# A fused block-causal attention and SoLU layer: two landing places for raw W_in, the gain taken into W_out's split, and 1/z by a diagonal matrix

## The chip, the cores and the metric

One core of one Trainium2 chip runs the whole program. The metric is device time in microseconds, the median of several executions. The engines are TensorE (PE, its weight loads PEld), VectorE (DVE), ScalarE (ACT), GpSimd (POOL), and SyncE (SP), which here only issues DMAs.

## The reference

Two stages, all inputs float32 (the launch hands W_in, W_out and g_ln over as float64 words, so their raw loads are twice as large):

```
scores = q @ k^T / 8                       # 8 batches x 8 heads, 576 x 576, head size 64
scores = where(query_block >= key_block, scores, -1e9)     # blocks of 64
attn   = exp(scores - max); attn = attn / (sum(attn) + 1e-9)
x      = attn @ v                          # heads side by side: 4608 tokens x 512
h      = x @ W_in                          # 512 x 1024
solu   = h * softmax(h)
ln     = (solu - mean) / sqrt(var + 1e-6) * g_ln
out    = ln @ W_out                        # 1024 x 512
```

## The kernel before

**Work.** Attention runs over 32 pairs of heads (four pairs a batch). Batch 0 is cut in two: part 0 (queries and keys 0 to 255, line 506 on) for its four pairs, then part 1 (the rest), so that the first 256 tokens are ready early. The program's pairs 0 to 3 are part 0, 4 to 7 part 1, 8 to 35 the other seven batches. The token stage runs over 36 tiles of 128 tokens: `moe` multiplies by W_in (24 matmuls, L798), forms the SoLU and the layer norm on DVE, ACT and POOL (the first vector step is the maximum at L804), and multiplies by W_out (24 matmuls, L863), after the rows have been transposed and split (`ch`, and the remainder `cl`, L855 for the first tiles). Every float32 operand of a large matmul is split into a high and a low part (`xh`, `xl`, `wih`, `wil`, `woh`, `wol`, `qh`, `ql`, `kh`, `kl`), and three matmuls stand for one.

**A pair.** Scores (L617, L623) land in PSUM, DVE takes the negative row maximum (`nm`, L652), ACT takes the exponential with its row sum `z` (L664), DVE forms `rz` = 1/z (L674, L675), and each block of `pb` is multiplied by it (L682 POOL, L683 DVE, L684 ACT: whichever the planner picks). Pairs 0 to 7 (`PEP`) then transpose `pb` on TensorE (L604) into PSUM, and it is copied out to `pt` (L464, L465); later pairs transpose on DVE and by DMA. The product with v is L710.

**Weights.** `prep` (L406 on) takes W_in and W_out apart, 512 columns at a time. One raw load of two pieces lands in `ub` (L402 for W_in, L398 for W_out), and each piece goes through about nine steps: low word to float (L414), clamp (L416 DVE, L417 POOL), scale (L418 to L420), shift and merge of the words (L421, L422), an add (L423, L424), for W_out the product with g_ln (L426), the high part (L429, L430), the remainder (L431, L432). All sixteen pieces share `ub`, so a load waits until both pieces of the one before it have been read. `qz` and `kz`, the landing places of q and k for later pairs, hold parts of batch 0's v and of its k and q at first, so their first loads (L511) wait for part 0's last product with v and for the first transposes.

**Order.** `Schedule` is a planner inside the program: each operation has modelled durations, alternatives on other engines and a due time made of the table `PARAMS`, and a list scheduler writes out one fixed order for each engine before anything runs. Every engine then executes its own list strictly in that order, waiting on semaphores; SP's list of DMAs too. Where the planner sees TensorE without work before 125 us of its own clock it puts in filler transposes of the identity (L352).

## Time and profile before

| | us |
|---|---|
| median of 3 runs (lowest, highest) | 707.98 (704.84, 710.37) |
| the profiled execution | 709.96 |
| its span, first to last instruction | 707.8 |
| TensorE busy in the span | 681.5 |
| VectorE, ScalarE, GpSimd busy | 553.1, 478.9, 368.7 |

The profiled execution is one run, 2.0 us above the median. Its span is 2.2 us shorter than its time. "Busy" on TensorE counts the fillers too, and matmuls overlap in their pipeline.

### The profile page before, as it was taken

What the parts mean: (1) busy time and instruction counts of PE and PEld (TensorE: products, weight loads), DVE (VectorE), ACT (ScalarE), POOL (GpSimd) and SP (SyncE); (2) the same over time, 40 slices, a digit from 0 to 9 for tenths busy, and PEclk for the clock granted to TensorE, in tenths of its full rate; (3) what the DMA queues carried; (4) which work ended last, traced back from release to release, by engine and by line L of the source; (5) the groups of instructions that cost most, each with busy time, mean ns of one, the idle gap of its engine ahead of it and who ended that gap; (6) DMA issues with size and microseconds to landing.
All of it is one profiled execution on the core that took longest, in us unless ns stands there. A gap on an engine that the chain in (4) does not pass through costs nothing.

```text
span 707.8 us, 14535 instructions
## 1 busy us (share of the span) xinstructions
PE 681.5 (96%) x4888; PEld 541.7 (77%) x4888; DVE 553.1 (78%) x1211; ACT 478.9 (68%) x1180; POOL 368.7 (52%) x591
## 2 busy tenths in 40 slices
PE   6888899999999899999999999999999999999997
PEld 5776777777777678777777777787878778888885
DVE  1889999996887888989798979898989883444442
ACT  2787998786676868686777767777777773444432
POOL 1247757647474465556555555655555543444432
PEclk9899999999999999999999999999999999999999
DMA  8944568969698889889898979798979766223121
GB/s 166 210 121 94 116 120 146 169 144 175 152 177 200 170 189 180 195 176 185 189 193 180 194 173 198 182 185 189 190 184 173 189 153 140 70 64 90 61 75 45
DMA packets 223435, 109.76 MB, mean 155 GB/s; under 512 B 186496, under 2 KB 202368, under 8 KB 223360
## 3 DMA queue, kind: packets, MB, share of 16 engines
q1 hardware_dynamic: 222320, 108.56, 74.8%
q8 instruction: 39, 0.64, 0.4%
q10 hardware_dynamic: 1040, 0.26, 0.2%
q14 instruction: 36, 0.29, 0.1%
HBM read 37.23 MB, written 9.44 MB: 66 GB/s over the span
## 4 chain that ended last, share of the span: by engine, by line
PE 66%; DVE 9%; DMA 9%; ACT 7%; issue 3%; SPq 3%; POOL 3%; DVEq 0%; POOLq 0%; ACTq 0%
PE ps L798 24%; PE ps L863 23%; PE ps L710 9%; PE ps L623 7%; DMA ub<-in_moe_w_in_dram 4%; ACT pb L664 3%; PE ps L617 2%; DVE nm L652 2%; DVE pb L690 2%; DMA kz<-in_k_dram 1%; DMA ct<-zb 1%; ACT pb L684 1%; SPq L511 1%; DMA vr<-in_v_dram 1%; DVE qz L582 1%
## 5 line engine op out<-in xcount | busy, mean ns | idle before, releaser
L664 ACT ACTIVATE pb<-ps,nm 128x512 f32<-128x512 f32 (+4 forms) x288 | 156.7, 563 | 44.2 <-DVE nm L652 43.7
L652 DVE TENSOR_REDUCE nm<-ps 128x1 f32<-128x512 f32 (+4 forms) x288 | 130.6, 504 | 0.1
L682 POOL TENSOR_SCALAR pb<-pb,rz 128x256 f32<-128x256 f32 (+4 forms) x106 | 60.2, 582 | 109.5 <-DVE rz L675 57.2
L690 DVE STREAM_TRANSPOSE pb<-pb 128x1536 f32<-128x1536 f32 (+1 forms) x56 | 102.9, 1838 | 9.5 <-ACT pb L684 6.7
L684 ACT ACTIVATE pb<-pb,rz 128x384 f32<-128x384 f32 (+4 forms) x171 | 91.4, 608 | 9.4 <-DVE rz L675 8.0
L710 PEld LDWEIGHTS ps<-pt,vr 128*64 128x64 f32 x1648 | 80.2, 137 | 19.3 <-issue 9.5
L710 PE MATMUL ps<-pt,vr 128*64 128x128 f32 (+1 forms) x1648 | 92.6, 269 | 0.0
L798 PE MATMUL ps<-wih,xh 128*128 128x512 f32 x288 | 82.9, 410 | 0.4 <-DVE ub L806 0.4
L863 PE MATMUL ps<-woh,ch 128*128 128x512 f32 x288 | 81.7, 405 | 0.0
L798 PE MATMUL ps<-wil,xh 128*128 128x512 f32 x288 | 79.3, 397 | 0.0
L863 PE MATMUL ps<-wol,ch 128*128 128x512 f32 x288 | 78.7, 395 | 0.0
L798 PE MATMUL ps<-wih,xl 128*128 128x512 f32 x288 | 78.7, 395 | 0.0
L863 PE MATMUL ps<-woh,cl 128*128 128x512 f32 x288 | 78.7, 395 | 0.0
L623 PE MATMUL ps<-kh,qh 64*128 64x128 f32 (+3 forms) x256 | 54.5, 385 | 12.0 <-ACT pb L664 9.1
L863 PEld LDWEIGHTS ps<-woh,ch 128*128 128x128 f32 x288 | 51.9, 188 | 18.5 <-issue 6.6
L798 PEld LDWEIGHTS ps<-wil,xh 128*128 128x128 f32 x288 | 54.8, 190 | 13.0
L863 PEld LDWEIGHTS ps<-wol,ch 128*128 128x128 f32 x288 | 54.2, 188 | 12.9
L798 PEld LDWEIGHTS ps<-wih,xl 128*128 128x128 f32 x288 | 54.2, 188 | 12.8
L863 PEld LDWEIGHTS ps<-woh,cl 128*128 128x128 f32 x288 | 54.2, 188 | 12.8
L798 PEld LDWEIGHTS ps<-wih,xh 128*128 128x128 f32 x288 | 52.2, 190 | 15.0 <-DVE ub L806 0.9
L841 ACT ACTIVATE ch<-ct 128x512 fp32r<-128x512 f32 x62 | 37.7, 624 | 36.6 <-DMA ct<-zb 31.6
L664 ACT ACTIVATION_READ_ACCUMULATOR pb<-ps,nm 128x1 f32 x288 | 60.8, 211 | 0.0
(123 smaller groups left out, 1284.2 us busy)
## 6 DMA issues: line engine op xcount, KB each, us to landing
pt<-pb SPq DMA_DIRECT2D x112, 400.0 KB, 6.2
ct<-zb SPq DMA_DIRECT2D x124, 128.0 KB, 2.6
out_dram<-ob SPq DMA_DIRECT2D x36, 256.0 KB, 2.6
vr<-in_v_dram SPq DMA_DIRECT2D x64, 128.0 KB, 4.0
kz<-in_k_dram SPq DMA_DIRECT2D x56, 144.0 KB, 3.9
qz<-in_q_dram SPq DMA_DIRECT2D x56, 144.0 KB, 4.5
ub<-in_moe_w_in_dram SPq DMA_DIRECT2D x8, 512.0 KB, 6.5
ub<-in_moe_w_out_dram SPq DMA_DIRECT2D x16, 256.0 KB, 3.2
```

The costliest lines, as they stand in the source:

```text
L511: SP.dma_start(dst[32 * g : 32 * g + 32].rearrange("p m (g d) -> p (m g) d", d=32), src[b0, ha + g - g % 2 : ha + g - g % 2 + 2, :, 32 * ( ...
L617: PE.matmul(t[:, 192 + k0 : 192 + k1], w_, x_[:, k0:k1], start=n_ == 0, stop=n_ == 2)
L623: PE.matmul(PS(sps[h])[:, off : off + 128 * (i_ + 1)], w_[half[h], 128 * i_ : 128 * i_ + 128], x_[half[h], 0 : 128 * (i_ + 1)], start=n_ = ...
L652: op("DVE", t_dve(wid[u]), lambda sp=sp, off=off, u=u: DVE.tensor_reduce(out=nm_[u], in_=PS(sp)[:, off : off + wid[u]], axis=AX.X, op=ALU. ...
L664: ACT.activation(dst, src, AF.Exp, bias=nm_[u], accum_out=z_[zg][:, zc : zc + 1])
L682: op("POOL", 0.836 * nn + 243, lambda b=b, zg=zg, zc=zc: POOL.tensor_scalar(out=puv(pb, b, pep), in0=puv(pb, b, pep), scalar1=rz_[zg][:, z ...
L684: ("ACT", t_act(nn, 133), lambda b=b, zg=zg, zc=zc: ACT.activation(puv(pb, b, pep), puv(pb, b, pep), AF.Copy, scale=rz_[zg][:, zc : zc + 1 ...
L690: op("DVE", 1.058 * 128 * (s1 - s0) + 86, lambda s0=s0, s1=s1: DVE.transpose(pb[:, :, s0:s1, :], pb[:, :, s0:s1, :]), r=[("P", i, b) for b ...
L710: PE.matmul(dst(PS(av)[half[h]]), w_, pt_[:, a0:a1, sl, :], start=start, stop=stop)
L798: PE.matmul(o_, a_[:, c, :], w_[:, c, s_], start=(si == 0 and c == 0), stop=(si == 2 and c == NKI - 1))
L841: op("ACT", t_act(512, 150), lambda c_=c_, h_=h_: ACT.activation(h_, c_, AF.Copy), r=["ct"], w=[("ch", hf)], key=key + K["ce"], alts=[("PO ...
L863: PE.matmul(o_, a_[:, c, :], w_[:, c, :], start=(hf == 0 and si == 0 and c == 0), stop=(hf == 1 and si == 2 and c == 7))
```

## The change

Three edits, and a new table of planner numbers.

1. Raw W_in loads go in turn to `ub` and to a second place, the slots 12 to 19 of the two `pb` buffers (which part 1 fills later). W_in's pieces take turns among four sets of temporaries (two of them in `pb` and `pt`) in place of two. The new table gives the last half of W_in the first due time.
2. The product with g_ln is no step of its own: the high part of W_out is written with the scale g_ln, and the remainder is T1 * g_ln - high in one instruction.
3. For pairs 0 to 7 the blocks of `pb` are no longer multiplied by 1/z. A matrix `dg` with 1/z on its diagonal is made per block row (identity times broadcast 1/z, L702 of the new file, on DVE or POOL), and TensorE's transposes become float32 matmuls with `dg` as the moving operand (L620 of the new file).

Beside these, part 1 no longer transposes q of the first 256 rows (four matmuls fewer a pair, and copies of 256 columns for 512).

```diff
+DGP = tuple(range(8))
...
 PARAMS = {
...
+    "x": 854.098, "h0": -147.594, "hs": 1139.434, "h": -51.86, "he": -142.998, "c": 105.783, "sq": -2.995,
+    "ct": -113.19, "ce": 111.289, "o": 2480.877, "oe": 4.124, "w0": 952.251, "w1": -125.07, "q32": 126.658,
...
-    wtmp = [(zb[:, 0:512], zb[:, 512:1024], ob[0]), (ctf[:, 0:512], ctf[:, 512:1024], ob[1])]
...
+    wtmp += [[(pbf[i][:, 20:24], [("P", i, LAST)])] + [(ptb[i][:, :, c : c + 4].rearrange("p b s n -> p b (s n)"), [("pt", i, s_) for s_ in range(c, c + 4)]) for c in (12, 16)] for i in range(2)]
...
-    raws = ub2.bitcast(U32)
+    raws = [x.bitcast(U32) for x in (ub2, pball[:, :, 12 * P : 20 * P])]
+    rawk = [[[("ub", i)] for i in range(2)], [[("P", i, (h, 3)) for h in range(2)] for i in range(2)]]
...
+        j_ = i // 2 % 2 if gcol is None else 0
+        dst, ks = raws[j_], rawk[j_]
...
-            op("SP", nd_ * 640, lambda: fetch(raws, src), w=[("ub", 0), ("ub", 1)], key=key, tail=1550, dma=3000)
+            op("SP", nd_ * 640, lambda: fetch(dst, src), w=ks[0] + ks[1], key=key, tail=1550, dma=3000)
...
+        scale = 1.0 if gcol is None else gcol
+        op("ACT", 520 if gcol is None else 613, lambda: ACT.activation(hi, T1f, AF.Copy, scale=scale), r=k1 + ([] if gcol is None else ["gt"]), w=[(name, "h")], key=key,
...
+            op("DVE", 602, lambda: DVE.scalar_tensor_tensor(out=lo, in0=T1f, scalar=gcol, in1=hi.bitcast(F32), op0=ALU.mult, op1=ALU.subtract), r=k1 + ["gt", (name, "h")], w=[(name, "l")], key=key, port=True)
...
-                    PE.transpose(PS(pt)[:, (s_ - c0) * P : (s_ - c0 + 1) * P], pb[:, s_, :], ident)
+                    o_ = PS(pt)[:, (s_ - c0) * P : (s_ - c0 + 1) * P]
+                    if diag:
+                        u = next(u for u in bs if soff[u] <= s_ <= soff[u] + u[1])
+                        PE.matmul(o_, pb[:, s_, :], dg[:, dcol(u), :], start=True, stop=True)
...
+                        eng.tensor_tensor(out=dg[:, d0 : d0 + n_, :], in0=ident[:, None, :].to_broadcast([P, n_, P]), in1=rz_[zg][:, z0 : z0 + n_, None].to_broadcast([P, n_, P]), op=ALU.mult)
...
-                for b in bs:
+                for b in () if diag else bs:
```

The built programs show how the orders move. On SP, from the sixth row of the program on, before:

```order
L402 DMA ub_125<-in_moe_w_in_dram 64x2x1024 x2
L398 DMA gt_76<-in_moe_g_ln_dram 32x8x1 x4
L522 DMA vr0_80<-in_v_dram 128x4x64 x2
L526 DMA vr0_80<-in_v_dram 64x2x64
L522 DMA vr1_81<-in_v_dram 128x4x64 x2
L526 DMA vr1_81<-in_v_dram 64x2x64
L402 DMA ub_125<-in_moe_w_in_dram 64x2x1024 x2
L484 DMA xt1_119<-in_k_dram 128x8x64
L484 DMA xt2_120<-in_q_dram 128x8x64
L484 DMA xt1_119<-in_k_dram 128x8x64
```

and of the change, from its twelfth row (the first rows are the same loads of q, k and v; `vr` and the first two of these k and q loads stand ahead of what is shown):

```order
L493 DMA xt1_118<-in_k_dram 128x8x64
L493 DMA xt2_119<-in_q_dram 128x8x64
L493 DMA kz_79<-in_k_dram 64x8x64
L493 DMA kz_79<-in_q_dram 64x8x64
L407 DMA pb_88<-in_moe_w_in_dram 64x2x1024 x2
L403 DMA gt_76<-in_moe_g_ln_dram 32x8x1 x4
L407 DMA ub_124<-in_moe_w_in_dram 64x2x1024 x2
L407 DMA pb_88<-in_moe_w_in_dram 64x2x1024 x2
L521 DMA qz_78<-in_q_dram 32x36x32 x4
L407 DMA ub_124<-in_moe_w_in_dram 64x2x1024 x2
L521 DMA kz_79<-in_k_dram 32x36x32 x4
L403 DMA ub_124<-in_moe_w_out_dram 32x2x1024 x4
```

The first load of W_in has moved behind the loads of v and behind all of batch 0's q and k; the second and third follow it at once; the fourth stands behind the first load into `qz`. On DVE, where it first meets W_in (before: its steps at L420 and L421 stand between part 0's first maxima):

```order
L652 TENSOR_REDUCE nm0_01_93<-ps5_66 128x1
L560 TENSOR_TENSOR kl0_85<-ps4_65,kh0_84 128x256
L465 TENSOR_SCALAR qh0_82<-ps4_65 128x256
L652 TENSOR_REDUCE nm0_00_92<-ps5_66 128x1
L561 SCALAR_TENSOR_TENSOR ql0_83<-ps4_65,qh0_82 128x256
L420 TENSOR_SCALAR ct_127<-ct_127 128x512
L421 TENSOR_SCALAR zb_126<-zb_126 128x512
```

and of the change:

```order
L702 TENSOR_TENSOR dg_135<-ident_67,rz1_0_115 128x512
L666 MEMSET ps5_66 64x2x64
L666 MEMSET ps2_63 64x2x64
L670 TENSOR_REDUCE nm0_01_92<-ps5_66 128x1
L670 TENSOR_REDUCE nm0_00_91<-ps5_66 128x1
L670 TENSOR_REDUCE nm0_11_96<-ps2_63 128x1
L670 TENSOR_REDUCE nm0_10_95<-ps2_63 128x1
L425 TENSOR_SCALAR pt1_90<-pb_88 128x4x128
L692 TENSOR_SCALAR z0_0_109,zsum_134<-z0_0_109 128x4
L693 RECIPROCAL rz0_0_113<-z0_0_109 128x4
```

DVE now takes the maxima of three of part 0's pairs before its first step on W_in (L425), not of half a pair; the third pair's 1/z stands right behind that step. On TensorE, at the first matmuls with W_in, before:

```order
L623 MATMUL ps2_63<-kl0_85,qh0_82 128x512
L623 MATMUL ps5_66<-kl0_85,qh0_82 128x512
L710 MATMUL ps4_65<-pt0_90,vr0_80 64x128 x6
L710 MATMUL ps3_64<-pt0_90,vr0_80 64x2x2x32 x8
L710 MATMUL ps3_64<-pt0_90,vr0_80 64x64 x10
L798 MATMUL ps0_61<-wih_72,xh0_121 128x512 x4
```

and of the change:

```order
L641 MATMUL ps4_65<-kl0_85,qh0_82 128x384
L641 MATMUL ps2_63<-kl0_85,qh0_82 128x384
L620 MATMUL ps3_64<-dg_135,pb_88 128x128 x3
L620 MATMUL ps5_66<-dg_135,pb_88 128x128 x3
L825 MATMUL ps1_62<-wih_72,xh0_120 128x512 x4
```

The first tile's matmuls stand behind the products with v of pair 4 alone, where they stood behind those of pairs 4, 5 and 6. Over the whole program TensorE's list has 73 fillers for 141, 88 transposes of q and k (L547) for 104, and 100 matmuls with `dg` for 100 transposes. Ahead of the first matmul with W_out (L863, now L890) it has one group of L617 (six matmuls), six of 512 columns and six of 256 columns of L623, and 26 of L710 fewer than before.

## Rows read from the trace of the kernel before

**Rows 1.** The page: the span, busy time (share) and instructions of the engines, and TensorE in 40 slices of the span, tenths busy.
```profile
span 707.8 us, 14535 instructions
PE 681.5 (96%) x4888; PEld 541.7 (77%) x4888; DVE 553.1 (78%) x1211; ACT 478.9 (68%) x1180; POOL 368.7 (52%) x591
...
PE   6888899999999899999999999999999999999997
...
```

**Rows 2.** Busy time by stretch: from and to, length, then for each engine busy us and instructions, then the granted clock of TensorE, the DMA engines' share and GB/s.
```profile
0.00:24.00 24.00, 15.80 (x130) 13.91 (x131) 9.42 (x30) 8.69 (x24) 5.04 (x16) 0.87 0.88 172
24.00:99.00 75.00, 66.32 (x673) 54.43 (x671) 67.25 (x193) 65.78 (x173) 43.50 (x64) 0.95 0.54 129
99.00:146.00 47.00, 45.09 (x357) 35.17 (x356) 45.47 (x101) 37.64 (x99) 29.61 (x43) 1.00 0.91 149
146.00:250.00 104.00, 100.65 (x751) 79.12 (x750) 84.58 (x188) 72.11 (x182) 58.76 (x96) 0.98 0.84 170
250.00:600.00 350.00, 349.81 (x2539) 275.93 (x2538) 301.20 (x652) 252.55 (x635) 192.02 (x316) 1.00 0.91 183
```

**Rows 3.** TensorE's fillers in the view by line: instructions, busy us and mean ns, idle time before them and what ended it; and from the timeline of TensorE (start, us) the first matmuls with W_out.
```profile
L352 PE MATMUL ps<-ident 128*128 128x128 f32 x141 | 21.2, 304 | 1.4 <-ACT pb L664 1.4
...
145.33 1.19 PE L863 MATMUL ps<-woh,ch 128*128 128x512 f32 x4
```

**Rows 4.** The chain of waits from 0 to 50 us: start, us, what. The first and the last of the four transfers of W_in.
```profile
6.79 9.69 DMA ub<-in_moe_w_in_dram
...
38.08 6.30 DMA ub<-in_moe_w_in_dram
```

**Rows 5.** Busy time by stretch as in rows 2, for the first 40 us and for DVE's stretch.
```profile
0.00:20.00 20.00, 11.80 (x111) 10.03 (x113) 5.43 (x17) 5.72 (x14) 2.86 (x14) 0.94 0.86 162
20.00:40.00 20.00, 18.84 (x174) 16.42 (x174) 17.12 (x55) 16.46 (x50) 6.33 (x6) 0.89 0.85 191
24.00:134.00 110.00, 99.41 (x922) 80.25 (x921) 101.95 (x267) 96.28 (x250) 69.33 (x101) 0.97 0.65 136
```

**Rows 6.** Timeline of DVE: start, us, instruction. The end of part 0's eighth maximum with the 1/z behind it, and the first remainder `cl` of a token tile.
```profile
24.16 0.18 DVE L675 RECIPROCAL rz<-z 128x4 f32<-128x4 f32 x1
...
133.53 0.68 DVE L855 TENSOR_TENSOR cl<-ps,ch 128x512 fp32r<-128x512 f32 x1
```

**Rows 7.** DVE's rows by line and form from 0 to 140 us: busy us and mean ns of one.
```profile
L652 DVE TENSOR_REDUCE nm<-ps 128x1 f32<-128x384 f32 x14 | 7.3, 545 | 0.0
...
L423 DVE CUSTOM_DVE_ANT_0 zb<-zb,ob 128x1024 uint16<-128x1024 uint16 x6 | 4.6, 765 | 0.0
...
L579 DVE SCALAR_TENSOR_TENSOR ql<-ps,qh 128x512 fp32r<-128x512 f32 x4 | 2.7, 680 | 0.0
...
L683 DVE TENSOR_SCALAR pb<-pb,rz 128x256 f32<-128x256 f32 x3 | 1.9, 642 | 0.0
L683 DVE TENSOR_SCALAR pb<-pb,rz 128x384 f32<-128x384 f32 x2 | 1.7, 851 | 0.0
...
L561 DVE SCALAR_TENSOR_TENSOR ql<-ps,qh 128x256 fp32r<-128x256 f32 x4 | 1.7, 415 | 0.0
...
L431 DVE TENSOR_TENSOR wol<-ct,woh 128x512 fp32r<-128x512 f32 x2 | 1.4, 696 | 0.0
...
L683 DVE TENSOR_SCALAR pb<-pb,rz 128x640 f32<-128x640 f32 x2 | 1.2, 610 | 0.0
```

**Rows 8.** Timeline of TensorE: twelve and thirteen transposes of `pb`, and sixteen records (eight matmuls, two records each) of batch 0's q and k transposes by plain float32 matmul with what follows them.
```profile
74.77 1.47 PE L604 MATMUL ps<-ident,pb 128*128 128x128 f32 x12
76.17 0.49 PE L623 MATMUL ps<-kh,qh 64*128 64x384 f32 x2
...
59.49 1.09 PE L537 MATMUL ps<-ident,xt 128*64 128x128 f32 x16 [1.36 <-ACT pb L664]
60.41 0.39 PE L537 MATMUL ps<-ident,kz 128*64 128x128 f32 x4
```

**Rows 9.** The chain of waits from 300 to 321 us: start, us, what.
```profile
315.80 2.90 PE ps L710 x52
318.70 1.01 PE ps L623 x12
319.72 0.99 PE ps L617 x6
```

**Rows 10.** Timeline of SP (start, us of issuing) and of TensorE: part 0's last product with v, and the first load into `qz` behind it.
```profile
76.94 0.92 PE L710 MATMUL ps<-pt,qz 128*64 128x128 f32 x12
...
77.89 2.99 SPq L511 DMA_DIRECT2D qz<-in_q_dram  x4
```

**Rows 11.** TensorE from 22 to 28 us: busy time by stretch (columns as in rows 2), and from its timeline the fillers.
```profile
22.00:24.00 2.00, 2.00 (x11) 2.00 (x10) 1.99 (x10) 1.54 (x7) 2.00 (x2) 0.50 1.01 215
24.00:26.00 2.00, 2.00 (x19) 2.00 (x18) 0.59 (x5) 0.93 (x6) 0.34 (x1) 0.91 1.14 214
26.00:28.00 2.00, 2.00 (x21) 2.00 (x19) 1.98 (x6) 1.97 (x6) 0.00 (x0) 1.00 1.23 278
...
20.61 7.59 PE L352 MATMUL ps<-ident 128*128 128x128 f32 x51
```

More of the change, by code (lines that the diff above doesn't have):

```diff
@@ L315 @@
     PAD = 8
-    pbt = [sb(f"pb{i}", [4, NSL * 32 + PAD]) for i in range(2)]
+    pball = sb("pb", [2, 4 * (NSL * 32 + PAD)])
+    pbt = [pball[:, i].rearrange("p (r n) -> p r n", r=4) for i in range(2)]
     pbs = [x[:, :, 0 : NSL * 32].rearrange("p r (s i) -> p r s i", i=32) for x in pbt]
@@ L416, in prep @@
-        op("DVE", 335, lambda: DVE.tensor_scalar(out=T2, in0=high, scalar1=TOP, scalar2=-TOP, op0=ALU.min, op1=ALU.max), r=[kr_], w=[k2], key=key, port=True,
+            op("SP", nd_ * 640, lambda: fetch(dst, src), w=ks[0] + ks[1], key=key, tail=1550, dma=3000)
+        high = raw[:, :, :, 1].bitcast(F32)
+        op("ACT", 570, lambda: ACT.activation(T3.bitcast(I32), raw[:, :, :, 0], AF.Copy, scale=2.0**-29), r=kr, w=k3, key=key,
+           alts=[("POOL", 640, lambda: POOL.tensor_scalar(out=T3.bitcast(I32), in0=raw[:, :, :, 0], scalar1=2.0**-29, scalar2=1.0, op0=ALU.mult, op1=ALU.mult), K["a_t3"])])
@@ L423, in prep @@
[L423 removed]
+        op("DVE", 335, lambda: DVE.tensor_scalar(out=T1.bitcast(U32), in0=T2.bitcast(U32), scalar1=3, scalar2=0x7FFFFFF8, op0=ALU.logical_shift_left, op1=ALU.bitwise_and), r=k2, w=k1, key=key, port=True)
+        op("DVE", 602, lambda: DVE.scalar_tensor_tensor(out=T1.bitcast(U32), in0=T2.bitcast(U32), scalar=0x80000000, in1=T1.bitcast(U32), op0=ALU.bitwise_and, op1=ALU.bitwise_or), r=k1 + k2, w=k1, key=key, port=True)
@@ L424, in prep @@
+        op("DVE", 602, lambda: DVE.tensor_tensor(out=T1.bitcast(I32), in0=T1.bitcast(I32), in1=T3.bitcast(I32), op=ALU.add), r=k1 + k3, w=k1, key=key, port=True,
            alts=[("POOL", 1225, lambda: POOL.tensor_tensor(out=T1.bitcast(I32), in0=T1.bitcast(I32), in1=T3.bitcast(I32), op=ALU.add), K["a_ai"])])
-        if gcol is not None:
-            op("ACT", 613, lambda: ACT.activation(T1, T1, AF.Copy, scale=gcol), r=[k1, "gt"], w=[k1], key=key,
-               alts=[("POOL", 588, lambda: POOL.tensor_scalar(out=T1, in0=T1, scalar1=gcol, scalar2=1.0, op0=ALU.mult, op1=ALU.mult), K["a_cg"]),
-                 ("DVE", 400, lambda: DVE.tensor_scalar(out=T1, in0=T1, scalar1=gcol, scalar2=None, op0=ALU.mult), K["a_lf"])], port=True)
@@ L565, in trans @@
             def trans(x, ps, tail):
-                for c in range(4):
-                    block(ps, c * P, raw0[x][:, 512 * c :])
+                for c in range(4 if tail else 2):
+                    block(ps, c * P, raw0[x][:, 512 * (c if tail else c + 2) :])
                 if tail:
```

64 lines of the change are left out of this document (37 added, 27 removed), and 11 rows, old and new, of the table PARAMS.

## The prediction

> **What bounds the kernel now.** I read the page first: TensorE is busy for 681.5 of 707.8 us, and its slices are full from about a fifth of the span on [rows 1]. The view by stretch says where it is not: from 250 to 600 us it is busy 349.81 of 350, but up to 146 us it lacks 8.2 + 8.7 + 1.9 = 18.8 us, and 3.4 more from 146 to 250 [rows 2]. Of the busy time before 146 us another 21.2 us are fillers, which compute nothing [rows 3]. So from the first matmul with W_out at 145.33 us [rows 3] the kernel is a list of TensorE work executed almost without a hole, and before it some 40 us of TensorE's time go by without program work. Everything that this change can win lies there; later, more load on DVE, ACT or POOL costs nothing while TensorE stays the last to be ready.
>
> What holds the start is the next view. In the chain of waits the first 44 us are four transfers of W_in into the one landing place, the first ending at 6.79 + 9.69 = 16.5 us, the last at 38.08 + 6.30 = 44.4 us [rows 4]. From 24 to 134 us DVE is busy 101.95 of 110 us, ACT 96.28, TensorE 99.41 including fillers [rows 5]: DVE is the fullest and the one that paces softmax and the weights. It gets to the first `cl`, which the first matmul with W_out needs, at 133.53 + 0.68 = 134.2 us [rows 6].
>
> **The sum in one line.** Let t be the time of the first matmul with W_out. Before, t = 145.3 and 707.8 - 145.3 = 562.5 us follow. The change alters what follows by work that it moves behind t, and alters t.
>
> *Moved behind t.* By the order, one group of L617 (0.99 us), six 512-column matmuls of L623 (0.9, an estimate from the 1.01 of twelve that move as many columns), six of 256 columns (0.55, an estimate by the same row) and 26 instructions of L710 (2.90) [rows 9] stand behind it that stood ahead: 5.3 us. So after = t + 562.5 + 5.3, and t must come before 140.0 us for any gain.
>
> *Where DVE now gets to.* Its first step on W_in stands behind the maxima of three pairs; it is held until the first load lands, and ACT and POOL have a first step of the same load in front of their next attention work. Ahead of that load's end SP now issues 3.47 MB of v, q and k (by the shapes in the order), and the load is 1.05 MB: 4.52 MB. At 162 GB/s for 20 us, 3.24 MB, and 191 behind [rows 5] it ends at 20 + (4.52 - 3.24)/0.191 = 26.7 us. Before, DVE stood at the like place (eight maxima and W_in's first pieces done, by the order and its rows' means the same 12.8 us of work) at 24.1 us [rows 6]. That is +2.6 us.
>
> *What DVE has to do from there to the first `cl`*, by the two orders and the means of [rows 7]. Gone: eleven multiplications by 1/z: seven as in the rows, 3 x 0.642 + 2 x 0.851 + 2 x 0.610 = 4.85, and four others, 1.6 by the same rates: -6.5. New: seven `dg`, of 512, 384 and 256 columns; the trace has no such instruction. Bounds are the 0.415 us of a 256-column product from PSUM and 0.765, the add of L423; I take L431, two operands in SBUF as here, 0.70 for 512 columns: 3 x 0.70 + 3 x 0.52 + 0.35 = +4.0 (bounds +2.9 to +5.4). The add moves to POOL eight times, -6.1; nine more remainders of weights are DVE's, +6.3. Q's remainder of 256 columns for 512, four times: -1.1. Eight fewer copies out of PSUM, by the 0.415 row: -3.3. Attention work that now stands ahead of that point (four maxima at 0.545, four products on k or q at 0.78 by L431's rate, less one 1024-column product of 1.2): +4.1. Clamps and scales, two fewer: -0.9. Together -3.5 us of row means, which at DVE's 102 busy of 110 are some 3 us of the clock; I take -2.7, since means of overlapped rows are a little long. The first `cl` then ends at 134.2 + 2.6 - 2.7 = 134.1, and t is about 134.5.
>
> *Can TensorE be there by then?* Before t it ran 126.5 us (the first three stretches less the 0.7 us behind 145.3) [rows 2], 21.2 of it fillers [rows 3]: 105.3. Gone are 16 transposes of q at (60.41 - 59.49)/8 = 0.115 [rows 8], -1.8, and the 5.3 above. The 100 matmuls with `dg` replace transposes at (76.17 - 74.77)/12 = 0.117 us; their price is bounded by that from below (+0) and by a plain float32 matmul from above, where two of 64 rows, run side by side, take 2 x 0.115 = 0.23 us [rows 8]. I take the upper end, the nearest row: +11.3. 73 fillers at 0.15 (21.2/141) are 11.0. Sum 120.5 us of 134.5, which leaves 14 us of idle time where 18.8 were. I hold that for likely: 8.2 of the 18.8 lie in the first 24 us, when the scores waited on an ACT that waited for W_in. So the matmuls with `dg` cost nothing where they stand; the cover is the fillers and the waits. Without that cover they and the rest cost 9.5 us.
>
> *Steps with one answer.* The gain in W_out's split takes seven products (L426) off ACT and one off POOL, about 5 us off engines that run beside DVE: 0, and slack for ACT. The shares on ACT and POOL shift over the whole program (casts of q and k to ACT, copies and remainders of `ch` and `cl` to POOL), under TensorE's 349.81 of 350: 0, plus or minus 1. In the tail one product moves from POOL to DVE and a copy stands behind another on ACT: 0, plus or minus 1.
>
> **Forecast.** 134.5 + 562.5 + 5.3 = 702.3 us of span, 5.5 less. The profiled execution took 2.2 us more than its span and lay 2.0 above the median, so span and median agree to 0.2: **702.5 us**. Within 1% is 700.9 to 715.1, about what this kernel's runs can tell from no change.
>
> **One place where the skill speaks.** The granted clock was 0.50 (1.2 GHz) from 22 to 24 us and 1.00 (2.4 GHz) from 26 to 28; in between TensorE ran fillers and nothing else, 51 transposes from 20.61 us on [rows 11]. So transposes did raise the clock here, and I give 68 fillers fewer and 100 matmuls for transposes no price by the clock. The Trainium skill, "TensorE: Matmul & The Clock Gate", Part 4: PE-mode transpose, says that transposes do not count as TensorE's activity in the same way and do not engage the fast clock. The row speaks against it; by the rule the matmuls with `dg` would keep the clock up where transposes don't.
>
> **Rivals.**
> 1. *DVE runs fuller and t comes earlier* (chance 0.18). ACT has less to do, and W_in's second and third loads are in flight while the first is taken apart. If DVE never waited between 26.7 us and `cl`, its 102 us of work less 2.7 would put t at 126.4: 694.2 of span, 694.5. For it: the chain of transfers into one place [rows 4] is broken up. Against it: 93% busy is already high, and TensorE would have to be idle for 6 us only. In this I count, at 0.03, that fewer stretches at 1.2 GHz shorten the way to t: a stretch of 2 us at 0.50 loses 1.0 us of full-speed work [rows 11], five such would be 5 us, so 697.5. That is what the skill's rule would give.
> 2. *W_in's fourth load comes late* (0.20), the slower side. SP issues in order, and the fourth load now stands behind `qz`, which waits for part 0's last product with v; before, that product ran at 76.94 us and the load was issued at 77.89 [rows 10]. I put that product at 45 to 50 us, and the load's end, 3 us of issuing and 8 of transfer later, at 56 to 61, when DVE's list reaches it (about 55 us). Each us beyond is one us of t, since attention is queued behind on DVE and ACT. From 5.5 us on the change is no gain. At twice that, t = 145.5 and the time 713.5; past 12.5 us it is slower by over 1%.
> 3. *The start is bound by TensorE, not by DVE* (0.10). If the 18.8 us of idle time stay, t = 120.5 + 18.8 = 139.3 and the time is 707.3: no change. Then the second landing place does not do what it is there for: the first load ends 10 us later than before, the last no earlier than 44 us.
>
> The forecast, t from 130 to 139 and 698 to 707 us, has 0.52. A third of it lies below 700.9. Faster by over 1%: 0.18 + 0.17 = 0.35. Slower by over 1%: half of rival 2, 0.10, and 0.01 for waits in the long middle: 0.11. Within 1%: 0.54. The range leaves out a tenth at each end: 694.5 to 713.5.
>
> **What would show it.** DVE's first step on W_in at 26 to 27 us behind a wait on the DMA; the first tile's matmuls with W_in near 70 to 75 us for 99; the first matmul with W_out at 134.5, not 145.3; TensorE idle 14 us before it; a row of L620 near 0.23 us, two records each; 250 to 600 us still full. The prediction is wrong if t is beyond 140, if DVE waits for the fourth load, or if TensorE has holes behind 146 us that it had not.

## The result: slower by 0.3% to 0.7%, and the profile after

The changed kernel takes 711.12 us (median of 20 executions, 707.81 to 714.36), the kernel before 705.84 us on the same chip (20 executions). The ratio is 1.0068, 95% interval 1.0050 to 1.0087; on a second chip it was 1.0031 [1.0008, 1.0054]. The forecast was 702.5 us. The profiled execution of the changed kernel took 711.06 us, so it lies at the median; the one shown of before took 709.96 and lies 4 us above the median of the 20.

The page of the changed kernel: span, busy time, TensorE in 40 slices [rows 1].
```profile
span 709.1 us, 14483 instructions
...
PE 682.3 (96%) x4888; PEld 544.0 (77%) x4888; DVE 560.9 (79%) x1215; ACT 457.0 (64%) x1149; POOL 351.0 (49%) x586
...
PE   8889898999999999999999999999989999999997
```
Busy time by stretch, columns as in [rows 2].
```profile
0.00:24.00 24.00, 21.40 (x224) 18.78 (x226) 9.01 (x35) 11.19 (x39) 1.60 (x12) 1.00 0.97 202
24.00:99.00 75.00, 66.25 (x593) 55.75 (x590) 67.84 (x175) 58.49 (x151) 39.79 (x58) 0.95 0.50 111
99.00:146.00 47.00, 41.76 (x355) 33.98 (x354) 45.52 (x99) 37.11 (x93) 24.15 (x38) 0.96 0.94 164
146.00:250.00 104.00, 102.58 (x761) 80.68 (x761) 88.11 (x196) 76.87 (x191) 50.96 (x92) 1.00 0.85 172
250.00:600.00 350.00, 345.35 (x2475) 270.15 (x2472) 307.95 (x659) 236.10 (x615) 190.36 (x322) 1.00 0.90 178
```
The first 24 us gained 5.6 us of TensorE. From 99 to 146 us it lost 3.3, and from 250 to 600 it is no longer full: 345.35 of 350 for 349.81. The 8 to the right of its middle is the slice from 514 to 532 us.

TensorE by line and from its timeline (start, us): matmuls with `dg`, last wait ahead of W_out, first matmuls with W_in (L825, before L798) and with W_out (L890, before L863) [rows 3, 8].
```profile
L620 PE MATMUL ps<-dg,pb 128*128 128x128 f32 x200 | 28.7, 294 | 6.5 <-ACT pt L473 4.2 <-POOL dg L702 1.1 <-DVE dg L702 0.7
```
```profile
66.22 1.17 PE L825 MATMUL ps<-wih,xh 128*128 128x512 f32 x4
...
74.47 4.51 PE L620 MATMUL ps<-dg,pb 128*128 128x128 f32 x38 [0.41 <-ACT pb L682]
78.91 0.44 PE L641 MATMUL ps<-kh,qh 64*128 64x384 f32 x2
...
126.93 1.20 PE L355 MATMUL ps<-ident 128*128 128x128 f32 x9 [1.36 <-ACT pb L682]
...
137.39 1.10 PE L890 MATMUL ps<-woh,ch 128*128 128x512 f32 x4
```
The first tile has its matmuls with W_in at 66.2 us (99.0 before). W_out's come at t = 137.4, for 145.3 before and 134.5 forecast; TensorE (L355 are its fillers, before L352) runs to it without a wait from 126.93 us on. So 571.7 us follow t, for 567.8 forecast.

DVE's first step on W_in, and the first `cl` [rows 6].
```profile
24.51 0.43 DVE L425 TENSOR_SCALAR pt<-pb 128x512 f32<-128x512 f32 x1 [4.23 <-DMA pb<-in_moe_w_in_dram]
...
136.57 1.26 DVE L882 TENSOR_TENSOR cl<-ps,ch 128x512 fp32r<-128x512 f32 x2
```

The largest hole behind t. TensorE stops for 2.29 us at 522.7 us, since ACT has not copied x out of PSUM (L473); on ACT that copy stands behind the cast of `ch` (L868), which waits for the transfer of `ct` (L860 on SP). Timelines of TensorE, ACT and SP, and SP's waits from 505 to 520 us (us in total, times, longest):
```profile
524.96 0.44 PE L641 MATMUL ps<-kh,qh 64*128 64x384 f32 x1 [2.29 <-ACT xt L473]
```
```profile
523.90 0.63 ACT L868 ACTIVATE ch<-ct 128x512 fp32r<-128x512 f32 x1 [3.90 <-DMA ct<-zb]
524.44 0.69 ACT L473 ACTIVATE xt<-ps 128x384 f32<-128x384 f32 x2
```
```profile
512.44 3.94 SPq L532 DMA_DIRECT2D vr<-in_v_dram  x2
...
517.86 2.52 SPq L860 DMA_DIRECT2D ct<-zb  x4
...
SPq L532 <- PE ps L825: 2.6, 2, 2.3
```
`zb`, which that transfer reads, was ready at 512.4 us, but SP stood at a load of v that waited 2.3 us for TensorE, and issued `ct` only at 517.9.

### The profile page after: what moved, and what is told of

Same layout as the page of the kernel before. It is cut to its first block, busy times and chain, and to the rows that moved or that the text cites. A ratio compares the mean times of both kernels' runs of the same rounds, so it can differ in the third digit from the quotient of the medians.

```text
span 709.1 us, 14483 instructions
## 1 busy us (share of the span) xinstructions
PE 682.3 (96%) x4888; PEld 544.0 (77%) x4888; DVE 560.9 (79%) x1215; ACT 457.0 (64%) x1149; POOL 351.0 (49%) x586
## 4 chain that ended last, share of the span: by engine, by line
PE 63%; DVE 13%; DMA 8%; ACT 5%; SPq 5%; issue 3%; POOL 2%; POOLq 0%; DVEq 0%; ACTq 0%
PE ps L825 22%; PE ps L890 22%; PE ps L737 8%; PE ps L641 7%; DVE nm L670 3%; DMA ct<-zb 2%; PE ps L635 2%; DMA pb<-in_moe_w_in_dram 2%; ACT pb L682 2%; DVE pb L717 2%; ACT pb L711 1%; SPq L860 1%; DMA ub<-in_moe_w_in_dram 1%; SPq L493 1%; PE ps L620 1%
## 5 line engine op out<-in xcount | busy, mean ns | idle before, releaser
L682 ACT ACTIVATE pb<-ps,nm 128x384 f32<-128x384 f32 (+4 forms) x288 | 157.3, 558 | 76.3 <-DVE nm L670 68.9
L670 DVE TENSOR_REDUCE nm<-ps 128x1 f32<-128x384 f32 (+4 forms) x288 | 132.9, 508 | 0.7
L737 PEld LDWEIGHTS ps<-pt,vr 128*64 128x64 f32 x1648 | 80.7, 137 | 21.0 <-issue 4.5
L737 PE MATMUL ps<-pt,vr 128*64 128x128 f32 (+1 forms) x1648 | 92.6, 269 | 2.2 <-issue 0.7
L872 POOL TENSOR_TENSOR cl<-ct,ch 128x512 fp32r<-128x512 f32 x59 | 75.9, 1290 | 26.2 <-ACT ch L868 15.5
L825 PE MATMUL ps<-wih,xh 128*128 128x512 f32 x288 | 83.2, 410 | 0.6 <-ACT pb L682 0.6
L890 PE MATMUL ps<-woh,ch 128*128 128x512 f32 x288 | 82.0, 407 | 0.4 <-ACT ch L881 0.4
L890 PE MATMUL ps<-wol,ch 128*128 128x512 f32 x288 | 79.4, 397 | 0.0
L709 POOL TENSOR_SCALAR pb<-pb,rz 128x256 f32<-128x256 f32 (+4 forms) x110 | 63.4, 592 | 31.9 <-DVE rz L693 14.2
L825 PE MATMUL ps<-wil,xh 128*128 128x512 f32 x288 | 78.8, 395 | 0.0
L890 PE MATMUL ps<-woh,cl 128*128 128x512 f32 x288 | 78.8, 395 | 0.0
L711 ACT ACTIVATE pb<-pb,rz 128x128 f32<-128x128 f32 (+4 forms) x142 | 71.4, 570 | 11.4 <-DVE rz L693 8.8
L825 PE MATMUL ps<-wih,xl 128*128 128x512 f32 x288 | 78.5, 394 | 0.0
L804 POOL TENSOR_TENSOR xl<-xt,xh 128x512 fp32r<-128x512 f32 (+1 forms) x40 | 50.3, 1265 | 32.5 <-PE ps L825 21.0
L825 PEld LDWEIGHTS ps<-wih,xh 128*128 128x128 f32 x288 | 50.6, 189 | 19.7 <-issue 8.4
L890 PEld LDWEIGHTS ps<-wol,ch 128*128 128x128 f32 x288 | 54.7, 190 | 13.0
L890 PEld LDWEIGHTS ps<-woh,cl 128*128 128x128 f32 x288 | 54.4, 189 | 12.9
L825 PEld LDWEIGHTS ps<-wil,xh 128*128 128x128 f32 x288 | 54.2, 188 | 12.8
L825 PEld LDWEIGHTS ps<-wih,xl 128*128 128x128 f32 x288 | 54.1, 188 | 12.8
L890 PEld LDWEIGHTS ps<-woh,ch 128*128 128x128 f32 x288 | 52.6, 190 | 12.5 <-ACT ch L881 0.7
L641 PE MATMUL ps<-kh,qh 64*128 64x128 f32 (+3 forms) x256 | 54.3, 379 | 6.4 <-ACT xt L473 3.0
## 6 DMA issues: line engine op xcount, KB each, us to landing
qz<-in_q_dram SPq DMA_DIRECT2D x56, 144.0 KB, 4.6
kz<-in_k_dram SPq DMA_DIRECT2D x56, 144.0 KB, 4.0
```

Of the source, the lines that this page charges most:

```text
L641: PE.matmul(PS(sps[h])[:, off : off + 128 * (i_ + 1)], w_[half[h], 128 * i_ : 128 * i_ + 128], x_[half[h], 0 : 128 * (i_ + 1)], start=n_ = ...
L670: op("DVE", t_dve(wid[u]), lambda sp=sp, off=off, u=u: DVE.tensor_reduce(out=nm_[u], in_=PS(sp)[:, off : off + wid[u]], axis=AX.X, op=ALU. ...
L682: ACT.activation(dst, src, AF.Exp, bias=nm_[u], accum_out=z_[zg][:, zc : zc + 1])
L709: op("POOL", 0.836 * nn + 243, lambda b=b, zg=zg, zc=zc: POOL.tensor_scalar(out=puv(pb, b, pep), in0=puv(pb, b, pep), scalar1=rz_[zg][:, z ...
L711: ("ACT", t_act(nn, 133), lambda b=b, zg=zg, zc=zc: ACT.activation(puv(pb, b, pep), puv(pb, b, pep), AF.Copy, scale=rz_[zg][:, zc : zc + 1 ...
L737: PE.matmul(dst(PS(av)[half[h]]), w_, pt_[:, a0:a1, sl, :], start=start, stop=stop)
```

## The experiments

All times are medians, all ratios are to the kernel before on the same chip. t is the first matmul with W_out in the profiled execution, "rest" its span less t. "Changed order" means that the planner's list is the changed kernel's, edited only as told. Only the runs without dg and with the old table have orders of their own, so their t and rest divide other work.

| run | median us | ratio [95%] | t | rest |
|---|---|---|---|---|
| kernel before, second profile | 705.44 (one) | | 144.0 | 559.3 |
| changed kernel | 711.12 | 1.0068 [1.0050, 1.0087] | 137.4 | 571.7 |
| changed kernel again | 709.89 | 1.0031 [1.0008, 1.0054] | 140.6 | 567.4 |
| transposes for dg | 715.87; 715.95 | 1.0098 [1.0061, 1.0134]; 1.0132 [1.0093, 1.0172] | 134.8; 137.2 | 571.4; 578.3 |
| transposes for dg, twice each | 711.07 | 1.0047 [1.0023, 1.0070] | 141.2 | 568.5 |
| ACT's copies of x first | 709.18 | 1.0018 [0.9997, 1.0040] | 138.6 | 568.5 |
| SP's ct first | 706.92 | 0.9989 [0.9971, 1.0007] | 138.9 | 566.6 |
| both | 707.79; 705.84 | 0.9987 [0.9962, 1.0012]; 1.0007 [0.9987, 1.0027] | 139.7; 138.9 | 568.1; 564.2 |
| before, both | 701.94; 704.58 | 0.9953 [0.9935, 0.9971]; 0.9954 [0.9937, 0.9971] | 142.1; 145.5 | 556.9; 557.9 |
| 50 transposes ahead of t | 724.05 | 1.0218 [1.0188, 1.0248] | 143.1 | 576.2 |
| before, 50 transposes ahead of t | 709.94 | 1.0025 [1.0008, 1.0042] | 149.2 | 559.1 |
| both, 50 transposes ahead of t | 717.06 | 1.0157 [1.0127, 1.0186] | 144.4 | 568.8 |
| both, transposes for dg | 707.87 | 1.0048 [1.0020, 1.0077] | 134.6 | 572.3 |
| both, q and k ahead of W_out's load | 714.49 | 1.0096 [1.0066, 1.0127] | 147.1 | 566.0 |
| without dg, new order | 733.30 | 1.0365 [1.0339, 1.0391] | 141.4 | 590.6 |
| changed code, old table | 742.94 | 1.0486 [1.0438, 1.0534] | 96.8 | 641.9 |

### Profiles and the first hole

**The kernel before, unchanged**, for a second profile.

> The kernel before, unchanged, to have a second profile of it: the one shown ran about 4 us above the median of its 20 times. Theory A (the start won, the middle lost): TensorE is busy for over 349 of 350 us from 250 to 600 us again, the first matmul with W_out stands at 145 +- 1, and the span is 704 to 706. Rival C (before has such holes as well, and the profile shown was a lucky one in the middle): 346 to 348 of 350.

Span 703.3, t 144.0, 348.59 us of TensorE from 250 to 600. The rest is 3.2 us shorter than in the profile that the forecast was made from; the part on both repairs shows what that was.

**The changed kernel, unchanged.**

> The changed kernel, unchanged, as the measure for the three runs beside it and to see its holes a second time. Theory A: the first matmul with W_out at 137 +- 2, the wait of TensorE near 522 us is there again, 345 to 347 us of TensorE from 250 to 600; 0.3 to 0.9% slower than before. If the wait near 522 us is absent while the time is the same, it was an accident of one execution and A falls for that place.

t came at 140.6, 3.2 us later than in the first profile, and the rest was 4.3 us shorter. The wait near 522 us is there, but 0.54 us long for 2.29. So that hole is a weak place that comes out long in one execution and short in another.

**ACT's copies first** (seven places; `od_` is the planner's list, `j` the place of the cast).
```diff
+        for o_ in [casts of ch on ACT]:
+            for x in [the next two operations on ACT]:
+                if x is not a copy out of PSUM (L473): break
+                od_.remove(x); od_.insert(j, x); j += 1
```

> The changed kernel in its own order, but at seven places ACT copies x out of PSUM (L473) before, not after, the cast of ch (L868) that waits for the transfer of ct. Theory A: the wait of TensorE at 522 us (2.3 us) and the fall of the clock behind it (some 2 us) go, and smaller ones of the same kind: 3 to 6 us less, 705 to 708. Rival (the hole is only moved: TensorE is held next by the softmax that stands behind the same cast on ACT): less than 1 us, and a hole of the same size within 10 us of the old one.

Ratio 1.0018; against the changed kernel's 1.0068 and 1.0031 on other chips that is 1 to 3.5 us less, too wide to tell 3 from 1. In its trace the hole at 522 us is gone.

**SP's ct first** (ten places).
```diff
+        for o_ in [transfers of ct on SP]:
+            while the operation before it on SP is a load of v (L532) or a store (L896), and zb is made earlier:
+                put o_ ahead of it
```

> The changed kernel in its own order, but at ten places SP issues the four transfers of ct ahead of the loads of v (and of a store of the output) that it issued first. Theory A, with its root: at 522 us ACT waited for ct because SP issued it only at 517.9, 5.4 us after zb was ready, behind loads of v; with ct first, ACT's wait for ct falls from 19.4 us to under 10 in all, the hole at 522 us goes without any change on ACT, and the time falls by 2 to 5 us. Rival (ct's wait was covered elsewhere and other waits come in its place, among them for v): within 1 us of the changed kernel.

Ratio 0.9989 for 1.0031 on the same chip: 3.0 us less, and the intervals don't meet. SP's timeline of this run at the same tile, and what ended ACT's waits at the cast (us, times; the changed kernel's row below it):
```profile
511.47 4.36 SPq L860 DMA_DIRECT2D ct<-zb  x4
```
```profile
  DMA ct<-zb: 10.0, 5
```
```profile
  DMA ct<-zb: 19.4, 9
```
`ct` is issued 6.4 us earlier, and no hole stands at 522 us (the longest one behind t is now 1.43 us at 544 us, ahead of the softmax). The root of the hole at 522 us is shown: `ct`'s place on SP.

### What the matmuls with dg cost

**Transposes for dg**, in the changed order.
```diff
-                        PE.matmul(o_, pb[:, s_, :], dg[:, dcol(u), :], start=True, stop=True)
+                        PE.transpose(o_, pb[:, s_, :], ident)
```

> The changed kernel in its own order, with the 100 matmuls with dg replaced by transposes with the identity at the same places. The 1/z of the first eight pairs is left out of the result; the vector products that make dg still run. Theory B (the price of these matmuls lies on the engine that bounds the end): 100 x (0.23 - 0.117) = 11 us of TensorE work go, less what idle time takes; the time falls by 7 to 11 us, to 700 to 704, and the first matmul with W_out comes at 127 to 131 for 137.4. My prediction's step (fillers and waits cover them): the time falls by 0 to 3 us and idle time before the first matmul with W_out grows by 8 to 11 us.

> The run with transposes for the 100 matmuls with dg once more (1/z of the first eight pairs left out), since its profiled execution (708.1 us) was the fastest of eight with a median of 715.9. If that median stands (a ratio to before of 1.006 to 1.014), the matmuls don't cost 10 us but save some, and the profile should show where: theory D, that TensorE then falls to 1.2 GHz more often (mean granted clock 0.985 or less for 0.99), on its way to the first matmul with W_out and behind it. If it comes out at 701 to 708, the first measurement was disturbed.

Theory B and my step both miss. t comes at 134.8 and 137.2 us, and yet the time grows: by 6.1 us on the chip where the changed kernel ran too (1.0132 for 1.0031). The second trace, taken near its median, shows where: two holes of 1.9 and 2.4 us behind t of the kind seen above, and one of 2.3 us at 231 us of another kind (the product with v, L737, waits for the transfer of `pt`). The chain of waits to the one at 531 us (start, us, what):
```profile
526.21 4.01 DMA ct<-zb
...
530.29 0.63 ACT ch L868
530.92 0.39 ACT xt L473
```
and TensorE's row at the end of it:
```profile
531.35 0.44 PE L641 MATMUL ps<-kh,qh 64*128 64x384 f32 x1 [1.90 <-ACT xt L473]
```

**Transposes twice each**, so that TensorE is busy as long as with dg.

> As the run with transposes, but each of the 100 is issued twice, so that TensorE is busy there for as long as with dg (0.23 us each), with transposes for matmuls (1/z of the first eight pairs left out). Theory D1 (it is the busy time that keeps the clock up): like the changed kernel, within 2 us, clock 0.99. Theory D2 (transposes don't count for the clock, as the Trainium skill has it in TensorE: Matmul & The Clock Gate, Part 4: PE-mode transpose): as slow as with single transposes or slower, 714 to 722, with a mean clock of 0.985 or less.

711.07, within 1.2 us of the changed kernel beside it. D2 is out: a hundred transposes more did not make it slower than single ones but 5 us faster, and the clock from 24 to 99 us was 0.98, for 0.91 with single ones and 0.95 with matmuls. Stretch 24 to 99 us of the run with single transposes (second) and with double ones:
```profile
24.00:99.00 75.00, 62.65 (x533) 48.59 (x531) 68.53 (x176) 60.13 (x154) 40.21 (x58) 0.91 0.48 112
```
```profile
24.00:99.00 75.00, 64.74 (x591) 52.81 (x588) 68.60 (x174) 59.13 (x153) 40.36 (x58) 0.98 0.49 110
```
That fits D1, but from 99 to 146 us the clock was lower with double transposes (0.89 for 0.93), so the clock alone is not shown to be the 5 us.

### Is it the edits or the order?

**Without dg** (the first eight pairs multiplied by 1/z as before; new table).
```diff
-DGP = tuple(range(8))
+DGP = ()
```

> The changed kernel without the products with dg: the first eight pairs are multiplied by 1/z on ACT, POOL and DVE as before, the table of numbers stays the new one, and the planner makes a new order. Theory B: TensorE has 8 to 11 us less work before the first matmul with W_out, but DVE, ACT and POOL have the products again; t falls below 137 only if TensorE set it; 702 to 707. Rival C (what counts is how well the table fits the work it was made for): t later than 140 and holes in the middle, 712 or more.

**Changed code with the table of before.**

> The changed code with the table of numbers of before (the one new number, for dg on POOL, as in the change), so the planner makes an order of its own. Rival C (the order that a table gives, not the three edits, sets the result): the same edits come out at 715 or more, as without dg (733), with waits of TensorE of 20 us or more behind its first matmul with W_out. If the edits themselves cost or win, it is within 3 us of the changed kernel.

733.3 and 742.9: rival C holds, though the holes are of many kinds. Stretches 146 to 250 and 250 to 600 us, first without dg, then with the old table:
```profile
146.00:250.00 104.00, 97.84 (x739) 75.36 (x738) 92.56 (x207) 74.08 (x194) 42.27 (x81) 0.98 0.82 168
250.00:600.00 350.00, 340.88 (x2454) 267.91 (x2454) 306.45 (x654) 238.26 (x618) 186.51 (x324) 0.99 0.86 180
```
```profile
146.00:250.00 104.00, 94.10 (x734) 74.00 (x731) 86.96 (x196) 73.28 (x197) 53.69 (x90) 0.95 0.89 173
250.00:600.00 350.00, 344.82 (x2507) 271.09 (x2507) 300.97 (x659) 248.30 (x633) 197.75 (x324) 1.00 0.92 182
```
The orders that came with these two edits cost 22 and 32 us, several times what the change itself moved. With the old table W_out even began at 97 us, 41 us ahead of the changed kernel, in the slowest kernel of all: t says nothing across orders.

### Shifting TensorE alone

**50 transposes ahead of t**, in the changed order and in that of before.
```diff
+                for _ in range(50 if t == 0 and hf == 0 else 0):
+                    PE.transpose(o_[:, 0:P], ident, ident)
```

> The changed kernel in its own order with 50 transposes that nobody reads, 5.8 us at 0.115, put on TensorE right ahead of its first matmuls with W_out. Theory E (behind that point other engines and SP's queue pace TensorE, so that an earlier start of this work is given back in waits): the time grows by 0 to 3 us over the changed kernel, to 710 to 713, and the time without program work behind that point falls by 3 us or more. Rival (TensorE is the bound behind that point, as my prediction had it): the time grows by 5 to 6 us, to 715 to 716.

> The kernel before with the same 50 transposes (5.8 us) at the same place. Theory E: before, TensorE comes to this point 3 to 7 us later than in the changed kernel and has few waits left behind it to give (7.8 us in the second profile, spread in small pieces), so that most is paid: 4 to 6 us, 711.5 to 713.5. If it is 0 to 2 us, TensorE was not the bound of the kernel before either, and the sum of my prediction stood on nothing.

E falls, and so does its rival. 5.8 us cost the changed kernel 11 to 13 us (1.0218 for 1.0031 to 1.0068), and the kernel before only 1.8. By what was put down ahead of that run, 0 to 2 us means that TensorE was not the bound of the kernel before either: t plus a constant, the form of the forecast's sum, does not hold even in its own order. The changed trace loses most in one hole of 2.15 us at 384.6 us and the slow clock behind it, and its chain is the same once more:
```profile
382.17 3.49 DMA ct<-zb
...
385.73 0.63 ACT ch L868
386.36 0.39 ACT xt L473
...
386.79 1.39 PE ps L641 x9
388.18 3.96 PE ps L892 x11
```
The last row is eleven matmuls of 512 columns, 0.36 us each; twelve take 2.81 at 508.6 us of the changed trace, where the clock is 1.00.

### Both repairs

> Both repairs of the changed kernel's order: SP issues ct ahead of v's loads at ten places, and ACT copies x out of PSUM ahead of the cast of ch at seven. Theory A: they mend the same waits from two ends, so that the sum is little more than SP's alone (0.4% under the changed kernel): 0 to 1.5 us less than that, a ratio to the kernel before of 0.996 to 0.999. If they were independent: 0.993 to 0.995.

Ratio 0.9987 and, on another chip, 1.0007: no better than SP's alone, which fits one repair from two ends. With it, the two shifts and the kernel before:

> The 50 transposes (5.8 us) ahead of the first matmuls with W_out, in the changed kernel with both repairs of its order. Theory F (one chain makes all the larger waits behind that point, whatever shifts TensorE: SP issues ct late, behind other transfers; the cast of ch waits for it on ACT and holds the copies of x out of PSUM behind it; TensorE runs out of work and its clock falls): with the repairs the time grows by no more than the 5.8 us over the repaired kernel, to 709 to 714, for 724 without them. Rival (the order breaks in other places too when it is shifted): 718 or more.

> Transposes for the 100 matmuls with dg (1/z of the first eight pairs left out), in the changed kernel with both repairs. Theory F: the 9.9 us of work that go are no longer given back in that chain; the time falls from 716 to 700 to 707, that is 1 to 8 us under the repaired kernel. Theory D1 (the time that TensorE is busy keeps its clock up, and that is why fewer us of matmuls are slower): still 712 or more, with a mean clock under 0.985.

> The repaired changed kernel once more, as the measure for the three beside it: a ratio of 0.997 to 1.000 to the kernel before.

> The kernel before with the same two rules on its order (SP issues ct ahead of v's loads or of a store of the output, ACT copies x out of PSUM ahead of the cast of ch). Theory F: its profile shown had one such wait too (2.1 us at 230 us, and the clock fell behind it), which comes in some executions: 1 to 4 us less, a ratio of 0.994 to 0.999, so that the change with repairs is no faster than before with them. Rival (before's order has no such weak place worth the name): 1.000 +- 0.001.

> The repaired kernel before once more, beside the last try to mend the changed one. If 701.9 of the first measurement holds, the ratio to the kernel before is 0.993 to 0.998 and it lies 3 to 5 us under the repaired changed kernel; theory H's best case would come within 1 us of it.

F holds for the kernel before. For the two shifts neither it nor its rivals hold: 717.06 lies between the 714 of F and the 718 of its rival, 707.87 between the 707 of F and the 712 of D1. Before with both repairs is the fastest kernel found, 0.9953 and 0.9954 on two chips, 3.3 and 3.7 us less, and it **beats both kernels**. Its stretch from 250 to 600 us is full to the last hundredth:
```profile
250.00:600.00 350.00, 350.00 (x2539) 276.55 (x2538) 297.67 (x636) 251.50 (x621) 194.49 (x314) 1.00 0.89 181
```
And the profile shown of before had the same hole, which is what makes its rest 3 us longer than the second one's. The chain of its waits at 230 us (L841, L464, L623 and L798 answer to L868, L473, L641 and L825):
```profile
225.22 4.19 DMA ct<-zb
...
230.05 0.61 ACT ch L841
230.66 1.04 ACT junk L816 x2
231.70 0.39 ACT xt L464
...
232.13 1.01 PE ps L623 x6
233.14 4.30 PE ps L798 x12
```
The transposes for dg are milder with the repairs, but not cured: they lie 0.41% above the repaired kernel, for 1.01% without repairs, and F's gain of 1 to 8 us did not come. The 50 transposes still cost 1.5%, 10.6 us (11 to 13 without repairs), where F allowed 5.8. So this chain is one of several places that break.

And the repairs take as much from before (0.47%) as from the changed kernel (0.2 to 0.8%). On one chip the repaired pair stands at 705.84 and 701.94: the change is still 3.9 us slower. The chain through `ct` is therefore a fault of both kernels and **not** what the change lost.

### The stop at 105 us

In every trace of the changed kernel TensorE stops for 2.4 to 5.6 us between 105 and 112 us. Ahead of that, SP waits 9.7 us (repaired kernel) for W_out's one landing place, with k and q behind. They were moved ahead of that load, with both repairs in place.
```diff
+        w_ = [the last load of W_out on SP]
+        od_.remove(w_)
+        od_.insert(od_.index(the load of qz behind it) + 1, w_)
```

> The changed kernel with both repairs, and SP issues the loads of k and q (L521) ahead of the last load of W_out (L403), which waited 9.7 us on SP for its one landing place and held them until 101.7 us, for the 91 us that the planner's time had. Theory H (this wait on SP makes the stop of TensorE between 105 and 116 us, 2.6 to 5.6 us and the fall of the clock): the first matmul with W_out comes 2 to 4 us earlier, at 135 to 137, and the time falls by 1 to 4 us. Rival (the stop comes from the split of W_out itself, whose steps stand ahead of the softmax on ACT and would now get their load 4 us later): TensorE stops for as long or longer, t stays at 138 or later, the time is the same or up to 4 us longer.

The rival holds, and by more than it said: t 147.1, 8.2 us later, time 714.5. For theory H the run says less: k and q came only 2.7 us earlier (issued at 99.0 us for 101.7), since SP waited 10.6 us for DVE (L598) to free their place, while the load of W_out went from 98.5 to 106.8 us. TensorE's and ACT's waits from 100 to 120 us (us in total, times, longest), the clock, and SP's timeline:
```profile
PE ps L355 <- ACT pb L682: 11.2, 1, 11.2
```
```profile
ACT zb L427 <- POOL zb L426: 8.8, 1, 8.8
```
```profile
112.00:120.00 8.00, 1.84 (x8) 1.84 (x9) 3.29 (x7) 5.16 (x16) 3.33 (x6) 0.50 0.88 251
```
```profile
101.93 4.79 SPq L521 DMA_DIRECT2D qz<-in_q_dram  x4
106.82 2.83 SPq L403 DMA_DIRECT2D ub<-in_moe_w_out_dram  x4
```
TensorE stopped for 11.2 us. ACT's list has a step of W_out's split (L427) ahead of the softmax (L682); with W_out's load issued at 106.8 us it stood still for 8.8 us, and the softmax with it. So the place of that step on ACT makes the long stop of this run. In the changed kernel it is a part of the stop only: in the two traces and the repaired one (its second run) ACT waited at L427 for 0.3, 3.0 and 0.2 us, and TensorE stopped for 3.2, 5.6 and 2.6. The other 2.4 to 2.9 us pass mostly while ACT works on its list up to the softmax (L832, L800, L682); no run takes them away. The second landing place, which only W_in has, does nothing for W_out.

Here 8.2 us at t cost 6 to 8 us by the ratios (1.0096 for 1.0007 and 0.9987), and the rest was 566.0, between the repaired kernel's 564.2 and 568.1. Where all engines come late together, the rest stays; where TensorE alone was shifted, in either direction, the changed order paid more. That fits an order laid out for one timing of the engines against each other. It is argued, not shown, and before's order, which lost only 1.8 us to the same 50 transposes, does not fit it.

## Why the prediction was wrong

The forecast was 134.5 + 562.5 + 5.3, plus the 0.2 between span and median: 702.5. The first profile gave 137.4 + 571.7, and its execution took 2.0 us more than its span: 2.9 + 3.9 + 1.8 are the 8.6 us. Over more executions with the same lists up to t (six of the changed kernel's order, four of before's) the medians of t are 138.9 and 144.7, so t gained 5.8 us where 10.8 were forecast. The two unedited kernels' rests are 569.6 and 560.9 in the mean of two each: 8.7 us more, where 5.3 were forecast. Net: 8.7 - 5.8 = +2.9 us, between the ratios measured (+2.2 and +4.8 us). The base moved too: before's median over 20 executions is 705.84, 2.1 us under that of the three runs that the forecast started from. That 711.1 lies inside the range given, 694.5 to 713.5, is luck: its upper end stood for rival 2, which did not come.

Behind t, the second profiles say what the 8.7 us are made of. Busy time from t to the end, columns as in [rows 2], before and changed:
```profile
144.01:703.30 559.29, 553.15 (x3738) 437.08 (x3736) 430.36 (x894) 365.77 (x890) 288.93 (x470) 1.00 0.77 159
140.59:708.00 567.41, 559.51 (x3807) 441.09 (x3806) 447.00 (x922) 355.10 (x880) 287.98 (x487) 1.00 0.77 159
```
TensorE is busy 6.4 us longer and idle 1.8 us longer (7.9 for 6.1). In the first profiles it is 6.6 and 2.7 us, in the mean of the repaired pairs 7.2 and 1.6. So most of it is TensorE's own work, and the holes are the smaller part.

Ahead of t, the reading that the first matmul with W_out waits for the first `cl` does not hold for the kernel before. There `cl` ended at 134.2 us [rows 6], and W_out followed 11.1 us later, because TensorE's own list ran without a hole from this wait on to 145.33:
```profile
132.15 0.88 PE L352 MATMUL ps<-ident 128*128 128x128 f32 x6 [0.55 <-ACT pb L664]
```
The forecast left `cl` where it was (134.1) and set t 0.4 us behind it. So its gain of 10.8 us at t was nearly the whole of this lag, and it rested on TensorE being there in time, point 1.

1. **"The matmuls with dg cost nothing where they stand": this step failed.** The price was right: 19 matmuls from 74.47 to 78.91 us are 0.234 each, for the 0.23 taken. So was the sum of busy time ahead of t: 120.7 us in the mean of the six traces, for 120.5. The cover was not: idle time was to shrink from 18.8 to 14 us, and it was 16.6 to 19.8. With transposes in their place t comes at 134.8, 137.2 and 134.6 us, in the median 4.1 earlier than 138.9: a third of their 11.7 us (100 x 0.117) was paid at t, and 4.1 is nearly all of the 4.4 that t missed. TensorE's busy time ahead of t is then 112.1 to 112.7 us, some 8 less, and its idle time 22.2 to 24.5, only 4 to 6 more. The 14 us of idle time that I counted as cover are partly waits right ahead of L620 (6.5 us), and in the first changed trace the chain of waits to t passes through L620 for 4.6 us (start, us, what):
```profile
86.36 2.86 PE ps L620 x12
...
92.91 1.77 PE ps L620 x14
```
Where TensorE waits and others wait for what it does next, its work lies on the path, not beside it. That the whole program still got slower without these matmuls is the other half: what was won at t was lost behind it.
2. **DVE's list, -2.7 us: wrong in sign.** From 24.8 us to t DVE was busy 104.5 us, where [rows 5] had 102.0 in the like stretch; with transposes for dg it was 104.0 to 104.9. Nine more remainders of weights took 8.3 us (fourteen in 11.8, five before in 3.5) for the 6.3 counted. Clamps and scales rose from 3.7 to 5.2 us, where 0.9 less was counted, and the adds that left DVE were six, 5.0 us, not eight. The five `dg` of that stretch took 4.2 us, what was counted for seven, though one of 384 columns took 0.996 us for 0.52. The load of W_in landed at 24.5, not at 26.7, which gives 2.2 us back.
3. **The start itself** went as forecast: the first load, four transfers not one behind another, TensorE at 21.4 of the first 24 us, the first tile's matmuls even earlier (66 us for 70 to 75). My rival 2, W_in's fourth load, did not come about. But what was won by 99 us was partly lost again from 99 to 146, at the stop near 105 us, of which W_out's split makes a part. The prediction saw W_out's steps only as work for DVE, not as a wait in ACT's list.
4. **"250 to 600 us still full": failed**, and with it the constant behind t. 345.35 and 347.22 of 350 in two traces, for 349.81 and 348.59. I priced the new table's order behind t at 0 +- 1 us because TensorE was full in one trace; beyond the moved work it cost 3.4. One chain, `ct` on SP, was found and mended, but it is in both kernels. Between the repaired pairs' rests, 566.1 and 557.4, 3.5 us are left beside the 5.3 moved: 1.6 of them are idle time of TensorE (their rows have 347.2 and 349.1 of 350 against 350.0 twice), and 1.9 busy time, the next point.
5. **The moved work, 5.3 us: too small.** TensorE's busy time behind t grew by 6.4 to 7.2 us, which alone eats the 5.8 that t gained. It is not the clock: in both second profiles the granted clock was 1.00 wherever TensorE was busy behind t. What takes the 1.1 to 1.9 us beyond the price no run singles out. One difference of the lists is large enough: behind t the changed one comes to matmuls with W_in or W_out from other work 68 times, that of before 56 times, and twelve of them take 2.99 us right behind scores and 2.81 behind their own kind (first changed trace):
```profile
505.60 2.99 PE ps L890 x12
508.59 2.81 PE ps L825 x12
```
Twelve times 0.18 would be 2.2 us; this is an estimate, argued and not shown.
6. **Rivals.** For t, rival 3 (chance 0.10) is the case that came: the 18.8 us of idle time stay (16.6 to 19.8), and t is 138.9 for its 139.3. Its reason, that TensorE and not DVE binds the start, holds in part: the chain of waits to t is TensorE's from 126.9 us on, and DVE's and ACT's from 118 to 126.9. W_in's first load ended 8 us later than before (24.4 for 16.5) and the last at 53.5 us, later than 44, as it said too; but the second place was of use: the first tile came 33 us earlier. Its time, 707.3, was still too low, since the constant behind t (points 4 and 5) fails there as well. That the prediction would fall if TensorE had holes behind 146 us it said itself.

## What to carry to other kernels

Where each engine runs a fixed list, a full engine in one trace is a property of that list and of its timing, not a bound that stays: price a new order behind the edit, not only in front of it. Before work is counted as covered by idle time, look which wait ends right ahead of it. And where a list has a cast that waits for a DMA, nothing that TensorE needs should stand behind it: putting such transfers first on SP and such copies first on ACT gave 0.5% on the kernel before, more than the three edits.
